# Moving bulk loads between small-matmul bursts and spacing four weight folds, in a linear-attention block bound by TensorE

## Chip, cores, metric

One core of one Trainium2 chip. The metric is the time of one execution on the device in microseconds (us), lower is better. The kernel before takes 834.03 us (median of 3 runs, 833.58 to 834.33).

## The reference, cut to what matters

```python
mod = silu(c) @ w_mod                       # six rows of 1024: sa, ca, ga, sb, cb, gb
h = layernorm(x) * (1 + ca) + sa            # S = 2048 tokens, D = 1024
q, k, v = split(h @ wqkv)                   # 32 heads of 32
pq, pk = phi(q), phi(k)                     # phi(t) = where(t > 0, t + 1, exp(t)) + 1e-6
kv = einsum('bhsd,bhse->bhde', pk, v)       # one 32 x 32 matrix a head, summed over all tokens
z  = sum of pk over the tokens
o  = (pq @ kv) / (pq . z + 1e-6)
x  = x + ga * (o @ wo)
h  = layernorm(x) * (1 + cb) + sb
x  = x + gb * ((silu(h @ w_gate) * (h @ w_up)) @ w_down)      # F = 3584
```

## The kernel before

The tokens are cut into four chunks of 512 (chunk 0 to chunk 3, `sc` in the code). In each chunk TensorE computes K and V in groups of eight 128x512 matmuls. Between K groups 1 and 2 of a chunk lies the **KV burst** of the chunk before: 128 small matmuls, 32 columns of weights each, which add `phi(k)` times V into PSUM. After chunk 3 comes a fourth burst, and then Q. KV is folded into `wo` there (four **folds** of 16 small matmuls), so that attention's output needs one product only (tile `a_ps`). VectorE meanwhile sums the rows of `w_mod` (`mod_step`, 1.2 us each), whose bulk loads come transposed by DMA (`mod_load`), and modulates the next chunk's layer norm `hT` (8 slices of 0.33 us).

The parts that the change touches; `# ...` marks cuts:

```python
    def mod_load(q, cols):                     # two transposing loads, 1 MB of SBUF each
        for h in range(2):
            t = big("wmt", [DC // 2, D])
            lo = q * D + h * NB
            last = nc.sync.dma_start_transpose(t[:], w_mod[:, lo:lo + NB])
            # ...
    K_STEPS = [(), (), (0, 2), (0, 2, 4, 5, 6)]   # w_mod sums behind these K groups, by chunk
    V_STEPS = [0, 4, 4, 7]                        # and behind V, in front of the hT modulation

    for sc in range(NSC):
        if sc > 0:
            k_phase(sc, 0, 2)
            kv_phase(sc - 1)                   # the burst
            if sc == NSC - 1:
                wo = [big("wo", [4, D]) for _ in range(2)]
                # ... eight loads of wo, issued behind the w_mod loads
            k_phase(sc, 2, 8)
        v_phase(sc)
        if sc + 1 < NSC:
            # ...
                ln1(sc + 1)                    # layer norm, then DMA transposes into hT
        # ...
        steps = mod_step(V_STEPS[sc], last_veps[0].ins if sc + 1 < NSC else None)
        if sc == NSC - 1:
            # ... wo is scaled by ga, behind `steps`
        if sc + 1 < NSC:
            with tc.issue_after(last_phi[0].ins):
                modulate_all(hTs[sc + 1], ca1T, saT)
        # ...
        if sc + 1 < NSC:
            with tc.issue_after(last_load[0].ins):
                last_load[0] = mod_load(*((2, gaT), (3, sbT), (4, cbT))[sc])

    # ... burst of chunk 3, KV copied out
    q_phase(1, 2, 4)
    # ... two transposes of KV
    den_sum(0)                                 # 32 small matmuls: the denominators of chunk 0
    den_spread(0)                              # their broadcast, by way of DRAM
    q_phase(1, 4, 6)
    fold_wo(0, 0)
    q_phase(1, 6, 8)
    fold_wo(0, 1)
    q_phase(2, 0, 2)
    fold_wo(1, 0)
    q_phase(2, 2, 3)                           # one group only
    fold_wo(1, 1)
    # ... later den_apply(0) and the a_ps tiles
```

Of the kernel before, what the change touches and what calls it, by code (L numbers as in the profile page):

```python
# [9 lines left out]
ALU = mybir.AluOpType  # L10
BF16 = mybir.dt.bfloat16
# [10 lines left out]
def kernel(  # L22
# [13 lines left out]
    nc = tc.nc  # L36
    P = nc.NUM_PARTITIONS
    _, S, D = A_x.shape
    F = B_w_gate.shape[1]
    DH = 32  # L40
    HPC = P // DH
    ST = S // P
    DC = D // P
# [3 lines left out]
    NSC = S // SCW  # L47
# [14 lines left out]
    wo_v = A_wo.rearrange("(h g i e) n -> h g e i n", h=2, g=4, i=HPC)  # L62
# [34 lines left out]
    def mm(out, lhsT, rhs, start, stop):  # L97
        return tc.keep_in_program_order(nc.tensor.matmul(out, lhsT=lhsT, rhs=rhs, start=start, stop=stop))  # L98

    def transpose(out, in_):  # L100
        return tc.keep_in_program_order(nc.tensor.transpose(out, in_, ident[:]))  # L101

    def big(name, shape):
        return k8.tile([P] + shape, BF16, name=name, tag="k8")

    def acc_a():
        return pa.tile([P, NB], F32, name="acc", tag="pa")

    def acc_b(name, shape=(NB,), dt=F32):
        return pb.tile([P] + list(shape), dt, name=name, tag="pb")  # L110
# [6 lines left out]
    last_load = [None]  # L117
# [70 lines left out]
    sbT = const.tile([P, DC], F32, name="sbT")  # L188
    cbT = const.tile([P, DC], F32, name="cbT")
    cb1T = const.tile([P, DC], F32, name="cb1T")  # L190
    gaT = const.tile([P, DH], F32, name="gaT")
    sc_row = const.tile([P, D], BF16, name="sc_row")
    ga_t = ep.tile([P, NB], F32, name="e")
    ga_bc = ga_t[:].bitcast(BF16)
# [4 lines left out]
    KVB = kvb[:, 0:HG * DH].rearrange("p (g e) -> p g e", e=DH)  # L199
    KVT = kvb[:, HG * DH:].rearrange("p (h e) -> p h e", e=P)  # L200
# [11 lines left out]
    last_veps, last_nmr = [None], [None]  # L212
# [78 lines left out]
    last_phi = [None]  # L291
# [12 lines left out]
    def k_mms(sc, gs, accs, cc_lo=0, cc_hi=DC):  # L304
        for cc in range(cc_lo, cc_hi):
            for (t, nb), acc in zip(gs, accs):
                mm(acc[:], lhsT=hTs[sc][:, cc, t * P:(t + 1) * P], rhs=wk[cc // 4][:, cc % 4, nb * NB:(nb + 1) * NB],
                   start=(cc == 0), stop=(cc == DC - 1))

    def k_evac(sc, gs, accs):  # L310
        for (t, nb), acc in zip(gs, accs):
            phi_to(pks[sc][:, t, nb * NB:(nb + 1) * NB], acc[:])

    def k_phase(sc, lo, hi):
        if lo == 0:
            pks[sc] = big("pk", [STC, D])
        for g in k_groups[lo:hi]:
            accs = [acc_a()]
            k_mms(sc, [g], accs)
            k_evac(sc, [g], accs)  # L320
            mod_step(int(k_groups.index(g) in K_STEPS[sc]))

# [13 lines left out]
    def q_phase(sc, lo=0, hi=DC, steps=0):  # L336
        if lo == 0:
            pqs[sc] = big("pq", [HG, SCW])
        for qc in range(lo, hi):
            acc = acc_a()  # L340
            for cc in range(DC):
                mm(acc[:], lhsT=wq[cc // 4][:, cc % 4, qc * P:(qc + 1) * P], rhs=hTs[sc][:, cc, :],
                                 start=(cc == 0), stop=(cc == DC - 1))
            phi_to(pqs[sc][:, qc, :], acc[:])
            mod_step(steps)
# [35 lines left out]
    ga_dram = dram.tile([1, D], BF16, name="ga_scratch")  # L381
    mod_steps = []

    def mod_load(q, cols):
        for h in range(2):
            t = big("wmt", [DC // 2, D])
            lo = q * D + h * NB
            last = nc.sync.dma_start_transpose(t[:], w_mod[:, lo:lo + NB])
            mod_steps.extend((t[:, i, :], cols[:, 4 * h + i:4 * h + i + 1]) for i in range(DC // 2))
        return last  # L390

    def mod_step(n, anchor=None):
        if n == 0:
            return
        scale = 1.0
        if anchor:
            one = small.tile([P, 1], F32, name="one", bufs=1)
            with tc.issue_after(last_nmr[0].ins):
                nc.gpsimd.memset(one[:], 1.0)
            scale = one[:]  # L400
        with tc.issue_after(anchor or last_phi[0].ins):
            for _ in range(n):
                rows, col = mod_steps.pop(0)
                last = nc.vector.scalar_tensor_tensor(out=rows, in0=rows, scalar=scale, in1=sc_row[:], op0=ALU.mult,
                                               op1=ALU.mult, accum_out=col)
        return last

    K_STEPS = [(), (), (0, 2), (0, 2, 4, 5, 6)]
    V_STEPS = [0, 4, 4, 7]

    def ga_spread():
        turned = small.tile([P, P], F32, name="dsum", bufs=1)
# [15 lines left out]

    rbs = {}

    def den_sum(sc):
        pq = pqs[sc]
        den = acc_b("den")
        for hg in range(HG):
            for q in range(STC):
                mm(den[32 * q:32 * q + 32, 0:P], lhsT=Zden[:, hg, :], rhs=pq[:, hg, q * P:(q + 1) * P],
                                 start=(hg == 0), stop=(hg == HG - 1))
        dsum = small.tile([P, P], F32, name="dsum", bufs=1)
        nc.vector.tensor_scalar_add(out=dsum[:], in0=den[:, 0:P], scalar1=DEN_EPS)
        rb = rbs[sc] = small.tile([P, P], BF16, name="rb", bufs=4)  # L440
        with nc.allow_low_precision("bf16 reciprocal multiplies bf16 phi(q)"):
            nc.vector.reciprocal(out=rb[:], in_=dsum[:])

    def den_spread(sc):
        rb = rbs.pop(sc)
        for q in range(STC):
            nc.gpsimd.dma_start(out=rden_dram[sc, :, q * P:(q + 1) * P], in_=rb[32 * q:32 * q + 32, :])
        rbc = big("rbc", [HG, SCW])
        rv = rden_dram[sc].rearrange("(h g) t -> h (g t)", h=HPC)
        for h in range(HPC):  # L450
            nc.gpsimd.dma_start(out=rbc[h * DH:(h + 1) * DH].rearrange("p g t -> p (g t)"),
                                in_=rv[h].unsqueeze(0).to_broadcast([DH, HG * SCW]))
        rbcs[sc] = rbc

    def den_apply(sc):
        pq, rbc = pqs[sc], rbcs.pop(sc)
        for k in range(4):
            ks = slice(2 * k, 2 * k + 2)
            nc.vector.tensor_tensor(out=pq[:, ks, :], in0=pq[:, ks, :], in1=rbc[:, ks, :], op=ALU.mult)

    nc.vector.memset(sel[:], 0.0)

# [72 lines left out]
    for sc in range(NSC):  # L535
        if sc > 0:
            k_phase(sc, 0, 2)
            kv_phase(sc - 1)
            if sc == NSC - 1:
                wo = [big("wo", [4, D]) for _ in range(2)]  # L540
                for h in range(2):
                    for g in range(4):
                        with tc.issue_after(last_load[0].ins):
                            nc.sync.dma_start(out=wo[h][g * DH:(g + 1) * DH, :, :], in_=wo_v[h, g])
            k_phase(sc, 2, 8)
        v_phase(sc)
        if sc + 1 < NSC:
            with tc.issue_after(last_on[nc.vector.engine] if sc == 0 else last_phi[-5].ins):
                ln1(sc + 1)
        if sc == 0:  # L550
            q_phase(0, 0, 6)
        steps = mod_step(V_STEPS[sc], last_veps[0].ins if sc + 1 < NSC else None)
        if sc == NSC - 1:
            with tc.issue_after(steps.ins):
                for cc in range(DC):
                    w = wo[cc // 4][:, cc % 4, :]
                    nc.vector.tensor_tensor(out=w, in0=w, in1=ga_bc, op=ALU.mult)
        if sc == 2:
            with tc.issue_after(last_veps[0].ins):
                ga_spread()  # L560
# [3 lines that stand above are left out]
        if sc == 0:  # L564
            q_phase(0, 6, 8)
        if sc + 2 < NSC:
            for st in range((sc + 2) * STC, (sc + 3) * STC):
                load_x(st, nc.sync)
        if sc + 1 < NSC:
            with tc.issue_after(last_load[0].ins):  # L570
                last_load[0] = mod_load(*((2, gaT), (3, sbT), (4, cbT))[sc])

    q_phase(1, 0, 1, 2)
    q_phase(1, 1, 2)
# [1 line left out]
    nc.vector.tensor_copy(out=KVB, in_=kv_acc[:, :, 0:DH])  # L576
    nc.vector.tensor_tensor(out=Zden[:], in0=kv_acc[:, :, DH:DH + 1].to_broadcast([P, HG, DH]),
                            in1=zmask[:], op=ALU.mult)
    q_phase(1, 2, 4)
    tpk = acc_b("tp", (2, P), BF16)  # L580
    for h in range(2):
        transpose(tpk[:, h, :], KVB[:, 4 * h:4 * h + 4, :].rearrange("p g e -> p (g e)"))
    nc.vector.tensor_copy(out=KVT, in_=tpk[:])
    den_sum(0)
    den_spread(0)

    def fold_wo(h, nb):
        ns = slice(nb * NB, (nb + 1) * NB)
        ps = [acc_b("wf") for _ in range(4)]
# [5 lines left out]
        for g in range(4):  # L595
            (nc.scalar.copy if g % 2 == 0 else nc.vector.tensor_copy)(out=wo[h][:, g, ns], in_=ps[g][:])  # L596

    q_phase(1, 4, 6)
    fold_wo(0, 0)
    q_phase(1, 6, 8)  # L600
    fold_wo(0, 1)
    q_phase(2, 0, 2)
    fold_wo(1, 0)
    q_phase(2, 2, 3)
    fold_wo(1, 1)

    h2Ts = {}
# [86 lines left out]

    q_phase(2, 3, 4)
    with tc.issue_after(last_phi[0].ins):
        den_apply(0)
    q_phase(2, 4, 6)
    for st in range(STC):
        wo_tile(st)  # L700
    q_phase(2, 6, 8)
# [27 lines left out]
    for b in range(FC // WDF):  # L729
        w = big("wd", [WDF, D])  # L730
# [38 lines left out]
```

## Time and profile before

| | |
|---|---|
| time, median of the 3 runs before the change was tried | 834.03 us |
| span of the profiled run | 831.7 us |
| PE busy | 820.7 us, 99% |
| granted TensorE clock | 1.0 |

The head of the page of the kernel before. Column 1 of the second line is the busy time of TensorE's matmuls (PE).

```profile
span 831.7 us, 11105 instructions
...
PE 820.7 (99%) x4502; PEld 379.3 (46%) x4581; DVE 344.8 (41%) x655; ACT 168.7 (20%) x253; POOL 64.4 (8%) x166
```

TensorE is the bound, and there is no second one near. 64 big matmuls take 13.81 us from start to start, 215.8 ns each; counted by their weight loads, 13.81 us is also the median of all stretches of 64 without small ones between, at a granted clock of 1.0. What the change goes for is the *excess*: the time from one start to another, less 215.8 ns for each big matmul between.

Two bursts in PE's timeline of the kernel before: the second (in chunk 2, at 90.31 us), then the third (in chunk 3, at 119.19). Columns: start, length, engine, line, operation, tiles, sizes, count, and the idle time before the group with what ended it. "issue" means that the engine waited for nothing that the profile shows. Some matmul records are missing: a group of 47 that begins after 0.16 us of "idle" is 48 whose first record is lost.

```profile
86.76 3.62 PE L98 MATMUL acc<-wk,hT 128*128 128x512 bf16 x16
90.31 1.22 PE L98 MATMUL kvp<-v,pk 128*32 128x64 bf16 x128
91.69 10.31 PE L98 MATMUL acc<-wk,hT 128*128 128x512 bf16 x47 [0.16 <-issue]
...
115.65 3.62 PE L98 MATMUL acc<-wk,hT 128*128 128x512 bf16 x16
119.19 1.37 PE L98 MATMUL kvp<-v,pk 128*32 128x64 bf16 x128
120.72 1.24 PE L98 MATMUL acc<-wk,hT 128*128 128x512 bf16 x5 [0.16 <-issue]
122.17 9.24 PE L98 MATMUL acc<-wk,hT 128*128 128x512 bf16 x42 [0.21 <-issue]
```

How to read it: behind the second burst the first recorded big matmul starts at 91.69, the lost one at 91.47, so the burst cost 91.47 - 90.31 = 1.16 us. (16 matmuls before it take 3.45 us, but the burst starts 3.55 behind them: 0.09 us more to switch.) The third burst is longer itself, and six big matmuls later the stream stops again for 0.37 us: 122.17 - 119.19 - 6 x 0.2158 = 1.69 us, 0.53 above the second. Nothing in the records of semaphores releases that stop.

The loads of the kernel before, from the timeline of the queue that issues them (column 2 is the time over which they were issued), and the modulation of chunk 2's hT on VectorE:

```profile
81.58 10.03 SPq L388 DMA_TRANSPOSE wmt<-in_w_mod_dram  x2
...
110.76 8.85 SPq L388 DMA_TRANSPOSE wmt<-in_w_mod_dram  x2
119.70 4.89 SPq L544 DMA_DIRECT2D wo<-in_A_wo_dram  x8
```

```profile
84.28 2.67 DVE L237 TENSOR_SCALAR hT<-hT,sca 128x512 bf16<-128x512 bf16 x8 [0.81 <-issue]
```

A pair of w_mod loads lies over the second burst and another, with wo's loads issued behind it, over the third. Instructions come by DMA as well. The page's table of queues has them, PE's in this line (packets, megabytes, share of 16 engines' span):

```profile
q8 instruction: 36, 0.59, 0.3%
```

That is 36 packets of 16,384 bytes. That they are PE's is read from the count: the trace has 9,083 matmuls and weight loads, 252 a packet, and from 222 to 826 us a packet comes every 27.4 us, in which PE starts 253 of them (mean of 22 such intervals, from the packet records of the trace file).

The folds of the kernel before, from PE's timeline (32*32 weights are the folds, `den` the denominators, `a_ps` the first output tile):

```profile
153.43 0.63 PE L98 MATMUL den<-pq,Zden 128*32 128x128 bf16 x32
154.22 3.40 PE L98 MATMUL acc<-hT,wq 128*128 128x512 bf16 x15 [0.16 <-issue]
157.55 0.43 PE L98 MATMUL wf<-wo,kvs 32*32 32x512 bf16 x16
...
165.77 1.90 PE L98 MATMUL acc<-hT,wq 128*128 128x512 bf16 x8
167.60 0.58 PE L98 MATMUL wf<-wo,kvs 32*32 32x512 bf16 x3
168.40 0.43 PE L98 MATMUL wf<-wo,kvs 32*32 32x512 bf16 x13 [0.23 <-DVE wo L596]
168.99 5.13 PE L98 MATMUL acc<-hT,wq 128*128 128x512 bf16 x23 [0.16 <-issue]
173.95 1.24 PE L98 MATMUL a_ps<-wo,pq 128*128 128x512 bf16 x5
```

Three folds cost about 0.47 us each. The fourth comes one Q group (8 matmuls) behind the third, stops after three matmuls for the copies of the third out of PSUM, and costs 168.77 - 167.60 + 0.09 to switch = 1.26 us (168.77 is the lost first matmul in front of 168.99).

### The profile page before, as it was taken

Reading aid. Unit: us, or ns where it says so; the run is one execution under the profiler, and the core shown is the slowest. Engines: PE = TensorE matmul, PEld = TensorE weight load, DVE = VectorE, ACT = ScalarE, POOL = GpSimd, SP = SyncE. Lnnn points to the kernel's source line nnn. Section 1 sums busy time; section 2 is a strip of 40 time slices with the busy share of each in tenths; the row PEclk is TensorE's granted clock in tenths of the full one; section 3 lists DMA queues with packets and bytes.
Section 4 is the critical chain, followed back from the end, with each engine's and each line's share of the span. In section 5 each row is a group of like instructions: output and inputs, shape, how many; then the busy total and the mean of one; then the engine's idle time right before and its main releaser. Section 6 shows DMA issues by size and latency. Waiting matters only on the chain.

```text
span 831.7 us, 11105 instructions
## 1 busy us (share of the span) xinstructions
PE 820.7 (99%) x4502; PEld 379.3 (46%) x4581; DVE 344.8 (41%) x655; ACT 168.7 (20%) x253; POOL 64.4 (8%) x166
## 2 busy tenths in 40 slices
PE   8999999999999999999999999999999999999998
PEld 4444444444444444444444444444444444444444
DVE  5757779896344335421111354211114431111122
ACT  3445343434111111101111110111111101111000
POOL 2101020110221101100000010000001100000000
PEclk9999999999999999999999999999999999999999
DMA  9793694229996635646343173753405529610011
GB/s 328 292 203 90 119 214 88 53 81 280 377 239 230 216 126 165 169 142 218 116 140 114 54 219 95 250 193 98 156 1 169 154 69 346 228 47 0 19 58 51
DMA packets 144100, 129.07 MB, mean 155 GB/s; under 512 B 58608, under 2 KB 124656, under 8 KB 143536
## 3 DMA queue, kind: packets, MB, share of 16 engines
q1 hardware_dynamic: 139968, 114.97, 46.5%
q0 software_dynamic: 3792, 12.98, 5.2%
q8 instruction: 36, 0.59, 0.3%
q10 hardware_dynamic: 288, 0.40, 0.1%
q14 instruction: 16, 0.13, 0.0%
HBM read 101.98 MB, written 12.72 MB: 138 GB/s over the span
## 4 chain that ended last, share of the span: by engine, by line
PE 98%; DVE 1%; issue 1%; ACT 0%; POOL 0%
PE acc L98 90%; PE a_ps L98 7%; PE kvp L98 1%; DVE stats L224 0%; PE mod_ps L98 0%; PE den L98 0%; ACT xn L234 0%; DVE wo L596 0%; PE tp L101 0%; PE wf L98 0%; DVE pq L298 0%; ACT eb L295 0%; POOL rstd L218 0%; DVE mv L225 0%; DVE veps L216 0%
## 5 line engine op out<-in xcount | busy, mean ns | idle before, releaser
L98 PE MATMUL acc<-h2T,wgu 128*128 128x512 bf16 x1756 | 385.7, 379 | 1.9
L98 PEld LDWEIGHTS <-wgu 128*128 128x128 bf16 x1792 | 175.3, 98 | 211.3
L665 DVE TENSOR_TENSOR gu<-acc,e 128x512 bf16<-128x512 f32 x112 | 77.4, 691 | 289.9 <-PE acc L98 278.8
L98 PE MATMUL acc<-wd,gu 128*128 128x512 bf16 (+2 forms) x908 | 195.2, 372 | 0.9
L664 ACT ACTIVATE e<-acc 128x512 f32<-128x512 f32 x112 | 66.9, 597 | 374.8 <-PE acc L98 363.4
L98 PEld LDWEIGHTS <-gu 128*128 128x128 bf16 x924 | 89.3, 98 | 104.5
L98 PEld LDWEIGHTS <-hT 128*128 128x128 bf16 x512 | 49.6, 98 | 59.9 <-issue 0.7
L686 DVE TENSOR_TENSOR e<-acc,gb_bc 128x512 f32<-128x512 f32 (+2 forms) x33 | 22.3, 675 | 131.7 <-PE acc L98 122.7
L98 PE MATMUL a_ps<-wo,pq 128*128 128x512 bf16 x250 | 56.9, 379 | 0.3
L98 PE MATMUL acc<-wk,hT 128*128 128x512 bf16 x251 | 56.3, 379 | 0.7 <-issue 0.5
L98 PE MATMUL acc<-hT,wq 128*128 128x512 bf16 x248 | 55.7, 379 | 0.8 <-issue 0.6
L98 PE MATMUL acc<-wv,hT 128*128 128x512 bf16 x249 | 55.5, 379 | 0.4
L295 ACT ACTIVATE eb<-acc 128x512 bf16<-128x512 f32 x64 | 37.9, 596 | 74.8 <-PE acc L98 70.5
L234 ACT ACTIVATE xn<-x,nmr,rstd 128x1024 bf16<-128x1024 f32 x16 | 19.8, 1240 | 126.0 <-POOL nmr L232 126.0
L633 POOL DMA_DIRECT2D x_scratch<-x x16 | 9.8, 615 | 378.2 <-DVE x L626 378.2
L98 PEld LDWEIGHTS <-pq 128*128 128x128 bf16 x256 | 25.1, 98 | 30.2
L98 PEld LDWEIGHTS <-wq 128*128 128x128 bf16 x256 | 24.6, 98 | 29.8 <-issue 0.9
L296 DVE TENSOR_SCALAR eb<-eb 128x512 bf16<-128x512 bf16 x64 | 18.4, 291 | 32.2 <-ACT eb L295 32.0
L218 POOL TENSOR_TENSOR rstd<-veps,neg_half 128x1 f32<-128x1 f32 x32 | 17.8, 556 | 102.5 <-DVE veps L216 90.9
L626 DVE TENSOR_TENSOR x<-a_ps,x_sb 128x512 f32<-128x512 f32 x32 | 22.1, 690 | 8.1 <-PE a_ps L98 7.4
L689 DVE TENSOR_TENSOR ob<-e,x1r 128x512 bf16<-128x512 f32 (+2 forms) x33 | 22.3, 675 | 1.0
L627 DVE BATCH_NORM_STATS2 stats<-x 128x6 f32<-128x512 f32 x32 | 22.2, 694 | 1.1
(88 smaller groups left out, 297.3 us busy)
## 6 DMA issues: line engine op xcount, KB each, us to landing
wgu<-in_B_w_gate_dram SPq DMA_DIRECT2D x28, 1024.0 KB, 7.9
wgu<-in_B_w_up_dram SPq DMA_DIRECT2D x28, 1024.0 KB, 8.3
x_sb<-in_A_x_dram SPq DMA_DIRECT2D x32, 256.0 KB, 5.8
x_scratch<-x POOLq DMA_DIRECT2D x16, 512.0 KB, 3.4
x1r<-x_scratch SPq DMA_DIRECT2D x31, 256.0 KB, 2.8
wd<-in_B_w_down_dram SPq DMA_DIRECT2D x7, 1024.0 KB, 6.2
rbc<-rden_scratch POOLq DMA_DIRECT2D x16, 256.0 KB, 7.3
out_dram<-ob SPq DMA_DIRECT2D x31, 128.0 KB, 1.7
```

The costliest lines, as they stand in the source:

```text
L98: return tc.keep_in_program_order(nc.tensor.matmul(out, lhsT=lhsT, rhs=rhs, start=start, stop=stop))
L218: nc.gpsimd.tensor_tensor(out=rstd[:, 0:n], in0=veps[:, 0:n], in1=neg_half[:].to_broadcast([P, n]), op=ALU.pow)
L234: nc.scalar.activation(out=dst, in_=src, func=ACT.Identity, bias=nmr[:], scale=rstd[:, 0:1])
L295: nc.scalar.activation(out=e[:], in_=acc, func=ACT.Exp)
L296: nc.vector.tensor_scalar(out=e[:], in0=e[:], scalar1=1.0, scalar2=PHI_EPS, op0=ALU.min, op1=ALU.add)
L626: nc.vector.tensor_tensor(out=x1[:, ns], in0=a_ps[:], in1=x_t[:, ns], op=ALU.add)
L627: nc.vector.bn_stats(out=stats[:, nb, :], in_=x1[:, ns])
L633: nc.gpsimd.dma_start(out=x1_dram[st * P:(st + 1) * P, :], in_=x1[:])
L664: nc.scalar.activation(out=sg[:], in_=ps[0][:], func=ACT.Silu)
L665: gm = nc.vector.tensor_tensor(out=guT[sc][f // GPT][:, f % GPT, :], in0=ps[1][:], in1=sg[:], op=ALU.mult)
L686: nc.vector.tensor_tensor(out=yt, in0=y_ps, in1=gb_bc[:, ns], op=ALU.mult)
L689: nc.vector.tensor_tensor(out=ob, in0=yt, in1=x1r, op=ALU.add)
```

## The change

The intent: put the four folds two Q groups apart, so that none waits for the PSUM copies of the one before; put the first denominators directly in front of the first fold, which saves a switch between big and small matmuls; and take the bulk loads off the third burst, with wo loaded behind the second burst and the last turned w_mod rows behind the third. Since w_mod's last rows arrive later, two sums move forward into chunk 1. The core of the diff (cuts marked by `# ...`):

```diff
+    def hold_back(tiles):                      # a tiny VectorE write, behind which the load must wait
+        with tc.issue_after(last_phi[0].ins):
+            for t in tiles:
+                nc.vector.memset(t[:, 0, 0:1], 0.0)
# ... mod_load(q, cols, held=False) calls it
-    K_STEPS = [(), (), (0, 2), (0, 2, 4, 5, 6)]
-    V_STEPS = [0, 4, 4, 7]
+    K_STEPS = [(), (2, 3), (0, 2), (0, 2, 4, 6)]
+    V_STEPS = [0, 4, 4, 6]
# ...
             kv_phase(sc - 1)
-            if sc == NSC - 1:
+            k_phase(sc, 2, 4)
+            if sc == 2:
                 wo = [big("wo", [4, D]) for _ in range(2)]
+                hold_back(wo)
                 # ... the eight loads of wo
-            k_phase(sc, 2, 8)
+            if sc == 3:
+                mod_load(4, cbT, True)
+            k_phase(sc, 4, 8)
# ... wo is scaled in front of the sums behind V, no longer behind them
-        if sc + 1 < NSC:
+        if sc + 2 < NSC:
             with tc.issue_after(last_load[0].ins):
-                last_load[0] = mod_load(*((2, gaT), (3, sbT), (4, cbT))[sc])
+                last_load[0] = mod_load(*((2, gaT), (3, sbT))[sc])
# ...
     q_phase(1, 2, 4)
     # ... two transposes of KV
-    den_sum(0)
-    den_spread(0)
-    q_phase(1, 4, 6)
+    q_phase(1, 4, 5)
+    den_sum(0, acc_a())
     fold_wo(0, 0)
-    q_phase(1, 6, 8)
+    den_spread(0)
+    q_phase(1, 5, 7)
     fold_wo(0, 1)
-    q_phase(2, 0, 2)
+    q_phase(1, 7, 8)
+    q_phase(2, 0, 1)
     fold_wo(1, 0)
-    q_phase(2, 2, 3)
+    q_phase(2, 1, 3)
     fold_wo(1, 1)
# ... q_phase(2, 4, 6) is issued behind den_apply(0)
```

More of the change, by code (lines that the diff above doesn't have):

```diff
@@ L382, with mod_load @@
     mod_steps = []
-    def mod_load(q, cols):
-        for h in range(2):
-            t = big("wmt", [DC // 2, D])
+    def hold_back(tiles):
+        with tc.issue_after(last_phi[0].ins):
+            for t in tiles:
+                nc.vector.memset(t[:, 0, 0:1], 0.0)
+    def mod_load(q, cols, held=False):
+        ts = [big("wmt", [DC // 2, D]) for _ in range(2)]
+        if held:
+            hold_back(ts)
+        for h, t in enumerate(ts):
             lo = q * D + h * NB
@@ L390, in mod_load, with mod_step @@
         return last
-    def mod_step(n, anchor=None):
+    def mod_step(n, anchor=None, behind_nmr=False):
         if n == 0:
@@ L395, in mod_step @@
         scale = 1.0
-        if anchor:
+        if behind_nmr:
             one = small.tile([P, 1], F32, name="one", bufs=1)
@@ L429, with den_sum @@
     rbs = {}
-    def den_sum(sc):
+    def den_sum(sc, den=None):
         pq = pqs[sc]
-        den = acc_b("den")
+        den = den or acc_b("den")
         for hg in range(HG):
@@ L458, in den_apply @@
             ks = slice(2 * k, 2 * k + 2)
-            nc.vector.tensor_tensor(out=pq[:, ks, :], in0=pq[:, ks, :], in1=rbc[:, ks, :], op=ALU.mult)
+            last = nc.vector.tensor_tensor(out=pq[:, ks, :], in0=pq[:, ks, :], in1=rbc[:, ks, :], op=ALU.mult)
+        return last
     nc.vector.memset(sel[:], 0.0)
@@ L543 @@
                         with tc.issue_after(last_load[0].ins):
-                            nc.sync.dma_start(out=wo[h][g * DH:(g + 1) * DH, :, :], in_=wo_v[h, g])
-            k_phase(sc, 2, 8)
+                            last_load[0] = nc.sync.dma_start(out=wo[h][g * DH:(g + 1) * DH, :, :], in_=wo_v[h, g])
+            if sc == 3:
+                mod_load(4, cbT, True)
+            k_phase(sc, 4, 8)
         v_phase(sc)
@@ L551 @@
             q_phase(0, 0, 6)
-        steps = mod_step(V_STEPS[sc], last_veps[0].ins if sc + 1 < NSC else None)
         if sc == NSC - 1:
-            with tc.issue_after(steps.ins):
+            with tc.issue_after(last_phi[0].ins):
                 for cc in range(DC):
                     w = wo[cc // 4][:, cc % 4, :]
-                    nc.vector.tensor_tensor(out=w, in0=w, in1=ga_bc, op=ALU.mult)
+                    scaled = nc.vector.tensor_tensor(out=w, in0=w, in1=ga_bc, op=ALU.mult)
+        mod_step(V_STEPS[sc], scaled.ins if sc == NSC - 1 else last_veps[0].ins, sc + 1 < NSC)
         if sc == 2:
@@ L578 @@
                             in1=zmask[:], op=ALU.mult)
-    q_phase(1, 2, 4)
-    tpk = acc_b("tp", (2, P), BF16)
-    for h in range(2):
-        transpose(tpk[:, h, :], KVB[:, 4 * h:4 * h + 4, :].rearrange("p g e -> p (g e)"))
-    nc.vector.tensor_copy(out=KVT, in_=tpk[:])
-    den_sum(0)
-    den_spread(0)
     def fold_wo(h, nb):
@@ L596, in fold_wo @@
             (nc.scalar.copy if g % 2 == 0 else nc.vector.tensor_copy)(out=wo[h][:, g, ns], in_=ps[g][:])
-    q_phase(1, 4, 6)
+    q_phase(1, 2, 4)
+    tpk = acc_b("tp", (2, P), BF16)
+    for h in range(2):
+        transpose(tpk[:, h, :], KVB[:, 4 * h:4 * h + 4, :].rearrange("p g e -> p (g e)"))
+    nc.vector.tensor_copy(out=KVT, in_=tpk[:])
+    q_phase(1, 4, 5)
+    den_sum(0, acc_a())
     fold_wo(0, 0)
-    q_phase(1, 6, 8)
+    den_spread(0)
+    q_phase(1, 5, 7)
     fold_wo(0, 1)
-    q_phase(2, 0, 2)
+    q_phase(1, 7, 8)
+    q_phase(2, 0, 1)
     fold_wo(1, 0)
-    q_phase(2, 2, 3)
+    q_phase(2, 1, 3)
     fold_wo(1, 1)
@@ L696 @@
     with tc.issue_after(last_phi[0].ins):
-        den_apply(0)
-    q_phase(2, 4, 6)
+        applied = den_apply(0)
+    with tc.issue_after(applied.ins):
+        q_phase(2, 4, 6)
     for st in range(STC):
```

## The prediction

> **What bounds the kernel.** TensorE. The page's first table: PE busy 820.7 of 831.7 us; the chain of waits is 98% PE; granted clock 1.0; PE's wait list sums to 4 us, most in the first 25 us, which the change doesn't touch. In the timeline 64 matmuls of 128x512 take 13.81 us start to start, 215.8 ns each. [...] About 3712 such matmuls, 801 us, stay. Only the excess around small matmuls can be won.
>
> **That excess, from the PE timeline** (start to start, less 215.8 ns per big matmul):
> - KV bursts (128 small matmuls, with re-entry): 1.26, 1.26, 1.79, about 1.26 us. The third, at 119.2 us, costs 0.53 us more: turned w_mod loads (issued 110.8 to 119.6, landed 118.1 and 123.1) and wo's eight loads lie across it. PE's instruction pages come by DMA too (table of queues: 36 packets, 16 KB each). A page came 0.7 us before the second burst, but 0.6 us after the third began. [...]
> - Folds of wo: about 0.47 us each for three, 1.29 for the fourth, which comes one query group after the third and waits for its PSUM copies ("PE wf <- DVE wo", 0.2 us, and a restart in the middle): 0.82 us more.
> - Transposes of KV with the first denominator sums: 0.78 us.
>
> **What the change does.**
> 1. Folds two groups apart: the fourth becomes like the others, -0.8 us.
> 2. Denominator sums directly before the first fold: one switch to 32-column matmuls (0.09 us) goes, -0.1 us.
> 3. wo loads after the second burst (estimate: issued 97 to 102 us), the last turned w_mod after the third (127 to 136): no bulk load on a burst, -0.5 us.
> 4. VectorE: two w_mod sums (1.2 us each) move from chunk 3 to chunk 1; four tiny memsets come; wo's scaling (4.9 us for 8) goes in front of the last six sums. Not on the critical path. By-products: denominators come about 1 us later, but their broadcast landed at 168.1 and is used at 172.3; chunk 2's hT transposes slip about 0.9 us against 2 us of margin (modulation starts 84.3, PE needs it at 86.8); chunk 3's queue behind wo's loads, which should be landed before xn is ready (102 to 109).
>
> Later PE only slides: gate/up weights are released by PE work, and no PE wait stands behind 170 us. The gain should survive: -1.4 us of 834.03.
>
> **Prediction:** 832.6 us; 831.8 to 834.0 in 8 of 10 cases. Faster by over 2%: 0.005; within 2%: 0.99; slower by over 2%: 0.005.
>
> **What would show it.** Span near 830.3. Third burst with an excess of 1.26 us, its instruction page fetched before it. Four folds of 0.47 us; the wait of PE wf for DVE wo gone. Denominators plus first fold under 1.2 us together. Pace 215.8 ns unchanged.
>
> **What would make it wrong.** hT of chunk 2 or 3 late, a PE wait at 86 or 115 us; the denominators' broadcast later than about 171 us, a wait at a_ps; the first gate/up weights (landed 203.1 and 206.1, needed 205.0 and 206.8) not moving with PE, which would take back up to 1 us; a new collision of burst and load; or the third burst's cost not being DMA but something that stays (then -0.9).

Its sum: -0.8 - 0.1 - 0.5 = -1.4 us of 834.03.

## The result, and the profile after

| | before | after |
|---|---|---|
| median, us (6 runs each, same chip) | 833.64 (833.46 to 834.33) | 833.33 (832.25 to 833.90) |
| ratio after / before | | 0.9993, 95% interval 0.9981 to 1.0006 |
| span of the profiled run | 831.7 | 831.0 |
| clock | 1.0 | 1.0 |

A ratio here and below is the mean time of one kernel's fast runs over the mean of the other's fast runs of the same rounds, so it is not quite the ratio of the medians quoted. The result lies inside the predicted range and within 2%, but the gain of 1.4 us is not there: the medians differ by 0.3 us.

The head of the page after:

```profile
span 831.0 us, 11112 instructions
...
PE 819.9 (99%) x4502; PEld 378.9 (46%) x4581; DVE 344.5 (41%) x659; ACT 168.5 (20%) x253; POOL 64.3 (8%) x166
```

PE's timeline after, at the same two bursts:

```profile
87.19 3.75 PE L98 MATMUL acc<-wk,hT 128*128 128x512 bf16 x16
90.87 1.22 PE L98 MATMUL kvp<-v,pk 128*32 128x64 bf16 x128
92.25 10.46 PE L98 MATMUL acc<-wk,hT 128*128 128x512 bf16 x47 [0.16 <-issue]
...
116.36 3.62 PE L98 MATMUL acc<-wk,hT 128*128 128x512 bf16 x16
119.91 1.22 PE L98 MATMUL kvp<-v,pk 128*32 128x64 bf16 x128
121.29 10.31 PE L98 MATMUL acc<-wk,hT 128*128 128x512 bf16 x47 [0.16 <-issue]
```

The third burst costs 121.29 - 0.22 - 119.91 = 1.16 us, as wanted. But around the *second* burst two groups became longer: the 16 matmuls in front of it take 3.75 instead of 3.62 us, and the 47 behind it 10.46 instead of 10.31. Together that is 0.29 us that was not there before.

PE's timeline after, at the folds (the denominators are named `acc` now, with `Zden`):

```profile
155.35 0.63 PE L98 MATMUL acc<-pq,Zden 128*32 128x128 bf16 x32
155.91 0.43 PE L98 MATMUL wf<-wo,kvs 32*32 32x512 bf16 x16
156.50 3.40 PE L98 MATMUL acc<-hT,wq 128*128 128x512 bf16 x15 [0.16 <-issue]
...
164.35 3.40 PE L98 MATMUL acc<-hT,wq 128*128 128x512 bf16 x15 [0.16 <-issue]
167.68 0.43 PE L98 MATMUL wf<-wo,kvs 32*32 32x512 bf16 x16
168.05 5.35 PE L98 MATMUL acc<-hT,wq 128*128 128x512 bf16 x23
173.24 2.11 PE L98 MATMUL a_ps<-wo,pq 128*128 128x512 bf16 x9
```

The fourth fold has one piece, 168.05 - 167.68 + 0.09 = 0.46 us, and the denominators with the first fold take 156.28 - 155.35 = 0.93 us. PE's wait for `wo` is gone from the list of waits. The list after is complete with three lines (us in total, times, longest):

```profile
PE mod_ps L98 <- DMA wme<-in_w_mod_dram: 1.8, 3, 1.1
PE acc L98 <- DVE sel L469: 1.2, 1, 1.2
PE acc L98 <- issue: 0.8, 5, 0.2
```

The first line is a wait of the start-up, in code that the change doesn't touch, and it was 0.5 us before. The loads and chunk 2's modulation after:

```profile
83.64 10.20 SPq L395 DMA_TRANSPOSE wmt<-in_w_mod_dram  x2
...
97.94 4.16 SPq L554 DMA_DIRECT2D wo<-in_A_wo_dram  x8
...
126.77 7.95 SPq L395 DMA_TRANSPOSE wmt<-in_w_mod_dram  x2
```

```profile
86.10 2.67 DVE L237 TENSOR_SCALAR hT<-hT,sca 128x512 bf16<-128x512 bf16 x8 [0.96 <-issue]
```

The modulation of chunk 2's hT starts 1.8 us later than before, 86.10 against 84.28 (PE itself stands 0.43 us later in this one trace, see the next table).

**A sum that closes.** In every trace the time from the first `a_ps` matmul to the end is 657.79 to 657.81 us. So the span is the start-up (to the first V matmul of chunk 0) + the stretch from there to `a_ps` + 657.80. In microseconds:

| | start-up | stretch | front of 2nd burst | 2nd burst | 3rd burst | folds |
|---|---|---|---|---|---|---|
| before | 30.25 | 143.70 | 0.09 | 1.16 | 1.69 | 4.62 |
| after | 30.68 | 142.56 | 0.23 | 1.32 | 1.16 | 3.72 |
| difference | +0.43 | -1.14 | +0.14 | +0.16 | -0.53 | -0.90 |

(Front: excess of the 16 matmuls before the burst. Burst: from its first matmul, less the big ones up to the end of any stop behind it. Folds: from the start of the fourth burst to `a_ps`, less its 96 big matmuls. The first burst is 1.16 everywhere.) The four parts sum to -1.13, the stretch.

### The profile page after: what moved, and what is told of

It is laid out like the page before. It is cut to its first block, busy times and chain, and to the rows that moved or that the text cites. A ratio compares the mean times of both kernels' runs of the same rounds, so it can differ in the third digit from the quotient of the medians.

```text
span 831.0 us, 11112 instructions
## 1 busy us (share of the span) xinstructions
PE 819.9 (99%) x4502; PEld 378.9 (46%) x4581; DVE 344.5 (41%) x659; ACT 168.5 (20%) x253; POOL 64.3 (8%) x166
## 4 chain that ended last, share of the span: by engine, by line
PE 97%; DMA 2%; issue 1%; DVE 0%; ACTq 0%; SPq 0%
PE acc L98 90%; PE a_ps L98 7%; DMA wme<-in_w_mod_dram 2%; PE kvp L98 1%; PE wf L98 0%; PE den L98 0%; PE mod_ps L98 0%; ACTq L126 0%; PE tp L101 0%; SPq L135 0%; DVE e L698 0%; DVE ob L701 0%
```

## The experiments

Two theories at first. **A:** the change gives its 1.4 us in every run, and chance in the start-up (+0.43 us in this trace) hides it. **B:** the change gives back part of its gain in chunk 2, where the modulation is now late. Within B three causes are mixed: the late hT itself; the w_mod loads, which are issued 2 us later than before (83.64 against 81.58) and now lie on the fetch of PE's instructions; and both together. The first four kernels shared one chip and 5 rounds (kernel before: median 833.89, 9 runs).

### after_again, before_again: the same two kernels once more

No edit.

> The changed kernel unaltered, for a second trace and more times. In its first trace the stretch from the first V matmul to the first a_ps matmul is 142.56 us against 143.70 before (-1.14: folds and denominators -0.90, third KV burst -0.53, chunk 2 around the second burst +0.29), but the first V matmul starts 0.43 us later (30.68 against 30.25) in code that the change does not touch. Theory A (the loss of gain is chance in the start-up loads): that stretch is again 142.5 to 142.7, the start of V differs from 30.68 and moves the time with it, and the mean over more rounds is about 1.1 us under before. Theory B (the change made chunk 2 unstable): the stretch itself varies by 0.5 us or more between traces, and the mean stays 0.2 to 0.4 us under before.

> The kernel before against itself: the noise of the method and a second trace. Ratio 1.0000 within 0.0006. The stretch from first V matmul to first a_ps again 143.70 within 0.1; the third KV burst again 0.5 us dearer than the others, its instruction page fetched after the burst began. The start of V (30.25 in the first trace) tells how much start-up varies: theory A says by 0.4 us or more, theory B by less than 0.2.

Measured: after 832.97 us (832.77 to 833.39), ratio 0.9989 [0.9975, 1.0002]; before 834.03, ratio 1.0000 [0.9988, 1.0013]. The traces say more than the times. PE's timeline of the repeated kernel after, at the second burst:

```profile
86.77 4.22 PE L98 MATMUL acc<-wk,hT 128*128 128x512 bf16 x16
90.91 1.22 PE L98 MATMUL kvp<-v,pk 128*32 128x64 bf16 x128
92.29 1.24 PE L98 MATMUL acc<-wk,hT 128*128 128x512 bf16 x5 [0.16 <-issue]
93.84 9.22 PE L98 MATMUL acc<-wk,hT 128*128 128x512 bf16 x42 [0.30 <-issue]
```

Here 0.60 us are lost in front of the burst and 0.46 behind it, at the same place as behind the third burst of the kernel before: six big matmuls behind the burst. The loss in chunk 2 is 1.06 us in this trace and 0.29 in the first, with the same code. In the repeated kernel before the third burst cost 2.24 us, not 1.69. Start-up was 30.26 and 30.22. The first trace lost less because PE itself stood 0.43 us later there (start-up 30.68), while hT was modulated at the same time in both (86.10 and 86.14). So the start-up does vary by chance (A has a part), but B has the larger: stretch 143.33 against 144.25, a gain of 0.92, where 0.91 (folds) + 1.07 (third burst) = 1.98 was earned and 1.06 given back.

### folds_only, loads_only: one half of the change each

folds_only is the kernel before with the new order of denominators and folds; loads_only is the kernel after with the old one (both keep the change's new order around `den_apply(0)`). loads_only against the kernel after:

```diff
+    q_phase(1, 2, 4)
+    # ... two transposes of KV
+    den_sum(0)
+    den_spread(0)
-    q_phase(1, 4, 5)
-    den_sum(0, acc_a())
+    q_phase(1, 4, 6)
     fold_wo(0, 0)
-    den_spread(0)
-    q_phase(1, 5, 7)
+    q_phase(1, 6, 8)
     fold_wo(0, 1)
     # ... the other two as before
```

> Before with only the regrouping on TensorE: first denominator sums in front of the first fold, folds two groups apart; loads and w_mod sums as before. If the account of the trace is right: -0.9 us in the stretch from the last KV burst to the first a_ps, nothing elsewhere, third burst still 0.53 us dearer; ratio about 0.9989. A rival reading, that regrouped folds only hand the wait on to a_ps, expects under -0.2 us.

> After with the folds and denominators as before: the moved loads and w_mod sums alone. If parts add up: fold stretch 4.62 as before, third burst 1.16, and chunk 2's loss of 0.29 to 1.06 us back: time between 0.3 us under before and 0.5 us over it, ratio 0.9996 to 1.0006. If instead folds and loads help each other, well under before (0.9990 or less).

Measured: folds_only 832.72 us against 833.89, 0.9987 [0.9974, 0.9999]: folds 3.72 us, second burst 1.16 with its front at 0.09, third burst 1.42. loads_only 834.06 against 834.11, 1.0000 [0.9986, 1.0013]: third burst 1.16, but the front of the second is 0.66 instead of 0.09 and the burst 1.90 instead of 1.16, 1.31 us lost. So the fold half keeps what it earns, and the half with the loads and sums is worth nothing as a whole: what it takes from the third burst it pays at the second.

### no_k1_sums: the kernel after without the two sums in chunk 1

```diff
-    K_STEPS = [(), (2, 3), (0, 2), (0, 2, 4, 6)]
-    V_STEPS = [0, 4, 4, 6]
+    K_STEPS = [(), (), (0, 2), (0, 2, 4, 6)]
+    V_STEPS = [0, 4, 4, 8]
```

> After without the two w_mod sums in chunk 1 (they go to the end of chunk 3). Theory: those 2.4 us of VectorE made chunk 2's hT late (0.13 us of TensorE stall) and pushed the turned w_mod load onto the second KV burst's instruction page (0.16 us). Then both stalls go: the stretch from first V to first a_ps is 142.27, the page of the second burst is fetched before it, and the time is 1.4 us under before, ratio about 0.9983. If theory B holds its spread of times is also as narrow as that of before (0.9 us), with A it stays as wide as after's (1.6 us). Rival: sums put back at the end of chunk 3 make the denominators or folds late, +0.3 us or more at the folds.

Measured: 832.08 us (831.89 to 832.52) against 833.89, 0.9978 [0.9966, 0.9991]. The second burst in PE's timeline:

```profile
86.71 3.62 PE L98 MATMUL acc<-wk,hT 128*128 128x512 bf16 x16
90.25 1.22 PE L98 MATMUL kvp<-v,pk 128*32 128x64 bf16 x128
91.64 10.31 PE L98 MATMUL acc<-wk,hT 128*128 128x512 bf16 x47 [0.16 <-issue]
```

Front 0.09, burst 1.16, stretch 142.26: nothing is lost. hT's modulation starts at 83.87. So the two sums are the root of the loss. The fetch of the page still came late (2.55 us behind the modulation, see below), but did no harm, so the share that I had given to the load was only half right.

### held3, no_k1_held3: the second pair of loads moved off the fetch

```diff
+            if sc == 1:
+                mod_load(3, sbT, True)         # behind K group 3 of chunk 1
             if sc == 3:
                 mod_load(4, cbT, True)
# ...
-        if sc + 2 < NSC:
+        if sc == 0:
             with tc.issue_after(last_load[0].ins):
-                last_load[0] = mod_load(*((2, gaT), (3, sbT))[sc])
+                last_load[0] = mod_load(2, gaT)
```

held3 keeps the two sums in chunk 1; no_k1_held3 has the edit of no_k1_sums as well.

> After, with both w_mod sums kept in chunk 1, but the turned w_mod load of chunk 1 moved between the first and the second KV burst (held back like the other two). This tells the two losses in chunk 2 apart. If the page of instructions is what the load delays: the second burst's excess falls from 1.32 and 1.62 to 1.16 us and its page starts before the burst. If the sums on VectorE make hT late: the stall of the first two K groups of chunk 2 (0.14 and 0.60 us above the 0.09 of the other chunks) stays, or grows, since hT's transposes now queue behind the load. Rival: one cause for both (the load alone, or the sums alone); then both go or both stay. Time 0.1 to 0.6 us over that of no_k1_sums.

> Candidate: no_k1_sums with the turned load of chunk 1 between the bursts too, so that no bulk load stands on any burst. All four bursts at 1.16 us, every page fetched before its burst or absent near it, hT of chunk 2 on time: stretch from first V to first a_ps 142.26 as in no_k1_sums, time 832.0, ratio 0.9978 to 0.9985. If hT's transposes queue behind the load, up to 0.5 us more.

Measured: held3 834.19 us against 834.11, 1.0001 [0.9988, 1.0014]; no_k1_held3 832.18, 0.9976 [0.9964, 0.9989]. held3 as a whole is no better, because hT comes still later: its transposes are issued at 77.92 to 83.79, behind the earlier loads on the same queue (issued from 69.5 to 77.8), where the kernel after issued them at 75.89 to 82.32. The last of them landed at 87.54 and the modulation started at 87.73. PE's timeline of held3:

```profile
88.20 4.37 PE L98 MATMUL acc<-wk,hT 128*128 128x512 bf16 x16 [1.28 <-DVE hT L237]
92.51 1.22 PE L98 MATMUL kvp<-v,pk 128*32 128x64 bf16 x128
```

PE stops 1.28 us for hT and then steps at the pace of the modulation (2.67 us for 8 slices, 0.33 each; 8 weight loads waited for it, 3.4 us in all). Yet behind the burst it lost nothing (1.16), although hT was later than in any other kernel. So a late hT costs PE in front of the burst by itself, but the stop *behind* the burst needs the load as well.

### collide2, collide3, collide4: the load on the fetch, with hT in time

All three have the edit of no_k1_sums, and hold the second pair of loads back behind a VectorE instruction: collide2 behind the last slice of chunk 2's modulation, collide3 and collide4 behind the sums in front of it. collide4 as it differs from the kernel after (collide3 issues it at its old place in the program):

```diff
+        summed = mod_step(V_STEPS[sc], ...)
+        if sc == 1:
+            mod_load(3, sbT, True, summed)     # hold_back behind `summed`
```

> no_k1_sums with the turned load of chunk 1 put onto the second burst on purpose: it is held back until chunk 2's hT is modulated (about 87 us), so its packets stand in the queues when the page for the second burst is asked for. VectorE's work before the burst is that of no_k1_sums. If loads delay the page: the page of the second burst starts 0.2 to 2 us after the burst, the burst costs 0.2 to 1.5 us more than 1.16, the first two K groups stay at 0.09, time up by the same amount. If the dear burst was VectorE's or late hT's doing: 1.16 us stays.

> Second try to put the turned load of chunk 1 onto the page of the second burst, with VectorE as in no_k1_sums. The first try issued it at 86.5 and 91.1 us and the page had already come at 87.5, before the packets: no collision was made. Here the load is held back behind the four w_mod sums beside V, about 83.5 us, so that it is issued at about 83.6 and 88 us, as in after, and lies in the queues when the page is asked for (about 88). If the load delays the page: hT of chunk 2 on time (0.09), the page 0.1 us or more after the burst's start, burst excess 1.3 to 2.0 instead of 1.16, the extra time at the one weight load in the K group behind the burst where after and loads_only stand too; time 0.2 to 0.8 us over no_k1_sums. If it was VectorE's sums or late hT: 1.16.

> Third try at the collision. In the second, the memset that holds the load back stood behind the modulation of hT on VectorE, so the load was issued at 86.2 and 90.9 us, again later than the page (87.2): no collision, 1.16. Now the memsets stand directly behind the four w_mod sums and the load should be issued at about 83.5 and 88 us, as in after. Expected as before: if the load delays the page, hT of chunk 2 on time (0.09), the page of the second burst at about the burst's start or later, its excess 1.3 to 2.0 with the extra time at the one weight load behind the burst; time 0.2 to 0.8 us over no_k1_sums. If VectorE's sums or late hT made the burst dear: 1.16 with a late load.

Measured: 831.88 us (0.9973 [0.9959, 0.9987]), 832.14 (0.9977 [0.9961, 0.9994]) and 832.13 (0.9978 [0.9961, 0.9994]), 3 rounds each, against 834.11, 834.06 and 833.86. The first two missed their design: their loads were issued at 86.5 and 86.2, but moved their first packets only 0.3 us after the page had begun (87.48 and 87.22, 1.1 us behind the modulation), so it went undisturbed. collide4 hit: loads issued at 84.10 and 88.20 and landed at 91.65 and 96.50 (after: issued 83.64 and 88.13), and the page came 2.38 us behind the modulation. But:

```profile
87.30 3.62 PE L98 MATMUL acc<-wk,hT 128*128 128x512 bf16 x16
90.85 1.22 PE L98 MATMUL kvp<-v,pk 128*32 128x64 bf16 x128
92.00 10.53 PE L98 MATMUL acc<-wk,hT 128*128 128x512 bf16 x48
```

Nothing is lost. So the load on the fetch isn't enough alone either. (no_k1_sums had said so already; collide4 says it with the load where the kernel after has it.)

### spacing_only, den_only: the two parts of the fold half

spacing_only is folds_only with the denominators at their old place; den_only is folds_only with the folds at theirs.

> Before with only the folds two query groups apart, denominator sums at their old place. From the trace: the fold stretch falls from 4.62 to 3.8 us (the fourth fold from 1.29 to 0.47), the wait of the fourth fold for VectorE's copies goes. If the denominators' place brought the gain, it stays above 4.4.

> Before with only the denominator sums in front of the first fold, folds spaced as before (one group between the last two). The fold stretch falls by 0.1 us, from 4.62 to about 4.5; the fourth fold keeps its wait. Rival: the grouping is worth 0.3 us or more.

Measured, one look each, state unknown: 833.21 and 834.43 us against 834.34. The traces decide: folds 3.82 and 4.52 us against 4.62. The spacing is worth 0.80, the denominators 0.10, both together 0.90; they add up, and they add to what the prediction had. den_only still has the wait of PE for `wo` (0.2 us), spacing_only has not.

### All traces side by side: when the instruction page comes

Eight bursts in the 14 traces have a stop behind them, always beside the seventh big matmul of the K group, that is 1.16 + 6 x 0.2158 = 2.45 us behind the burst's start. Behind the third burst (five traces of the old loads) the seventh weight load is late, behind the second (three traces) the instruction after it, the seventh matmul. Neither has a semaphore wait in the trace. Count the weight loads (all are recorded, each with one matmul): 1,978 instructions lie before the late one at the third burst and 1,467 at the second, and one more instruction of PE, a semaphore wait, is recorded between the two (at 111.8 us in the kernel before). So the two places are 512 instructions apart, about two packets at 252 recorded instructions each. That fits a wait for the instruction queue, and its 16,384-byte packets show for which of them (their times are from the packet records of the trace files; no view of the profile lists them). In the table, "page" is the start of the packet's record behind the end of hT's last modulation of that chunk, and behind the start of the burst; "cost" is the burst's excess above 1.16.

| kernel, burst | packets of a turned w_mod load in flight | page behind hT's end | page behind burst's start | cost |
|---|---|---|---|---|
| held3, 2nd (sums in chunk 1) | no | +1.07 | -1.03 | 0 |
| no_k1_held3, 2nd | no | +1.05 | -2.42 | 0 |
| after, 3rd | no | +1.04 | -1.77 | 0 |
| no_k1_sums, 2nd | yes | +2.55 | -1.16 | 0 |
| collide4, 2nd | yes | +2.38 | -1.40 | 0 |
| before, 2nd | yes | +2.66 | -0.70 | 0 |
| folds_only, 2nd | yes | +3.27 | -0.01 | 0 |
| after, 2nd | yes | +2.26 | +0.16 | 0.16 |
| folds_only, 3rd | yes | +3.40 | +0.41 | 0.26 |
| before, 3rd | yes | +3.19 | +0.58 | 0.53 |
| after_again, 2nd | yes | +2.75 | +0.65 | 0.46 |
| spacing_only, 3rd | yes | +3.28 | +0.65 | 0.79 |
| loads_only, 2nd | yes | +2.99 | +0.89 | 0.74 |
| before_again, 3rd | yes | +3.73 | +0.92 | 1.08 |
| den_only, 3rd | yes | +3.94 | +1.32 | 1.46 |

Two things are read from it. With no turned load in flight the page comes 1.0 to 1.5 us behind hT's end (all such cases at the second and third bursts, those not listed too; in collide2 and collide3 the load moved its first packet after the page had begun); with one in flight 2.3 to 3.9. The first bursts belong to the former: the tail of a w_mod pair still moved packets there, up to 1.05 us behind hT's end (kernel after), but none when the page began, 1.0 to 1.4 us behind. And the burst pays once the page begins later than the burst does, about as much as it is later. With page starts at or before -0.01 no trace shows a cost. In the eight stops the late instruction starts 2.3 to 2.6 us after the record of the page begins. The packet itself takes 0.9 to 1.2 us at these bursts with and without a load, so with a load in flight the fetch started later, but was not slower.

For the second burst the experiments fill a square:

| | sums in chunk 1: hT late | no sums in chunk 1: hT in time |
|---|---|---|
| load over the fetch | 1.32, 1.62, 1.90 (after, after_again, loads_only) | 1.16, 1.16 (no_k1_sums, collide4) |
| load moved | 1.16 (held3) | 1.16 (no_k1_held3) |

The late hT puts the page later by its own 1.8 us, the load by another 1.2 to 1.9 (+2.26 to +2.99 against held3's +1.07), and only both together miss this burst. Measured from hT's end: where hT is late PE waits for it, and the burst begins 2.10 us behind it in all four traces; with hT in time the second burst begins 3.3 to 3.8 us behind. A page that comes 1.0 to 1.5 us behind is early for both, one that comes 2.3 to 3.3 us behind only for the latter. At the third burst of the old loads the space is 2.6 to 3.0 us although PE does not wait for hT (front 0.09), and the load alone is enough: the page came 3.2 to 3.9 us behind.

**The best version** is the kernel after without the sums in chunk 1 (no_k1_sums): 832.08 us, where the kernel before had 833.89 and the kernel after 832.97 in the same rounds. The ratios of no_k1_held3, collide2, collide3 and collide4 (0.9973 to 0.9978) can't be told from its own 0.9978.

## Why the prediction was right or wrong

The prediction said 832.6 us, 831.8 to 834.0, and "within 2%" at 0.99. 833.33 lies in the range, but that says little: a range that ends at 834.0 holds a kernel without any gain, too, and the forecast gain of 1.4 us was 0.3 in these runs. Point by point:

1. **"Folds two groups apart: the fourth becomes like the others, -0.8 us."** Right: -0.80 in spacing_only, and the wait of PE for `wo` disappeared in each kernel with the new spacing.
2. **"Denominator sums directly before the first fold ... -0.1 us."** Right: -0.10 in den_only, and the sum -0.90 in every trace with both.
3. **"no bulk load on a burst, -0.5 us."** The mechanism was right: in each trace with the moved loads the third burst is 1.16 and its page begins 1.6 us or more before it. The size was read from one trace. The five traces that still have those loads show 0.53, 1.08, 0.79, 1.46 and 0.26 above 1.16, mean 0.82. "No bulk load on a burst" was not true of the second, over which a w_mod pair stays; that is the next point.
4. **"chunk 2's hT transposes slip about 0.9 us against 2 us of margin."** This step failed, and it is why the net gain is smaller than 1.4. Both numbers were wrong. The modulation slipped 1.8 us (84.28 to 86.10; 1.4 against PE's stream in that trace, 1.8 to 2.2 in after_again, whose start-up was not late, against the two traces of the kernel before), since the two sums of 1.2 us stand on VectorE in front of chunk 2's layer norm and all that hangs on it. And the margin was not from the first slice (86.8): PE needs slice 8 seven matmuls later, at 86.76 + 7 x 0.216 = 88.27, and the modulation takes 2.67, so it has to start by 85.6, 1.3 us behind 84.28. This rule fits the other traces: after, after_again and loads_only miss their limit by 0.07, 0.53 and 0.49 us, and the front of the burst lost 0.14, 0.60 and 0.57. Further, the prediction had listed a PE wait at 86 us from a late hT, and "a new collision of burst and load", as what would make it wrong, but not that the late hT would move the page and so make the collision. It cost 0.29, 1.06 and 1.31 us in the three traces that have the sums and the load over the fetch.
5. **"Not on the critical path"** for the other moves: right. The denominators' broadcast landed 1.5 us later (169.61 against 168.12) and in time, chunk 3's hT was not late, and gate/up's weights moved with PE: `a_ps` to the end is 657.80 us in all kernels.

The traces' sum is then, for the kernel after: -0.90 folds, -0.53 to -1.07 third burst, +0.29 to +1.06 second burst. The pairs of traces give -1.14 and -0.92 of stretch, on top of which the start-up adds chance: 29.84 to 30.79 us in fourteen traces of the same start-up code, +0.43 in the first pair. Theory A may so explain part of why the first 6 runs showed only -0.3 us (one execution of each kernel was profiled, so the start-up of the others is not known); theory B, that the change itself gives back, is shown by no_k1_sums, which takes back the sums alone and gains 0.9 us on after_again.

What stays open. Why the page comes 1.0 to 1.5 us behind hT's modulation where no turned load is in flight isn't shown, nor why it comes 2.3 to 3.9 us behind with one in flight; no run here separates the causes. For the third burst of the kernel before, the w_mod loads and wo's were never moved apart; but in all five traces of the old loads wo's first packets (2,048 bytes) moved after the page had begun (the closest is den_only: page 120.52, wo 120.84), so wo's packets did not delay its start, and the w_mod pair is left. What varies in the start-up was not looked for.

## What to carry to other kernels

When one engine is the bound (here PE, busy 99% of the span), look at the small stops that carry no semaphore, and compare the times of its instruction-page packets with them: a bulk transposing load in flight, or a late input that stops the engine just before, may each be harmless and together cost a microsecond (at the second burst here: 1.16 us with either alone, 1.32 to 1.90 with both). In these traces the space between the end of the last input's modulation and the burst decided it (2.1 to 3.0 us was too short with a load in flight, and 3.3 us just enough). Before moving spare work of another engine to an "idle" place, compute the slack from the *last* slice that the busy engine needs, not from the first, and count all that is queued behind the moved work. One trace gives a size with no error bar: the same stop measured 0.26 to 1.46 us in five traces.
